# Two-layer GELU network on one core: the order of the first chunk's products, the order of waits, and w1's loads cut into more pieces

## The chip, the core and the metric

The kernel runs on one core of one Trainium2 chip. Its time is the device time of a run in microseconds (us); the time of a kernel is the median of its runs. A profile is one further execution, recorded by the hardware profiler. TensorE is called PE in the profile's rows (its weight loads PEld), VectorE DVE, ScalarE ACT, GpSimd POOL, SyncE SP; a q behind an engine's name is its queue of issues.

## The reference

```
h = einsum("bsd,df->bsf", x, w1) + b1
h = gelu(h)                      # tanh approximation
out = einsum("bsf,fd->bsd", h, w2) + b2
```

All arrays are bf16: x is 1 x 2048 x 448, w1 448 x 1792, w2 1792 x 448; out is 1 x 2048 x 448. So there are 2048 tokens, a model width of 448 = 3 x 128 + 64, and a hidden width of 1792 = 14 x 128.

## The kernel before

The tokens are worked in four chunks of 512. For each chunk, layer 1 makes g = gelu(x w1 + b1) with the hidden width on the partitions, 14 F-tiles of 128 in 7 pairs (`Layer1`, one object a pair); then layer 2 multiplies g with w2 (`Layer2`) and VectorE adds b2 on the way out of PSUM.

Every product uses half of TensorE's rows, 64, and products of the two halves are issued one after the other, so that they run side by side. For a pair of F-tiles the "a" products take one half of the rows for each F-tile, the "b" products the other half. The 448 rows of w1 are three slices (k = 0, 1, 2) of 128 and 64 last rows, which stand in a tile of their own, `w1r`, where VectorE copies them to the other half for the odd F-tiles (line 411, event `w1rU`). So a pair has 6 a products, 6 b products of the slices (`b_main`) and 2 of the last rows (`b_last`), after which ScalarE applies GELU (line 279). A pair accumulates in one of four PSUM units, used in turn; a unit is taken again when ScalarE has read it. `mm` (line 221) records every product. When the half changes within a bank, it adds a wait for the product before it in that bank.

x must be turned so that its width lies on the partitions. For chunks 1 to 3 DMA transposes do that. For chunk 0 TensorE does: x is loaded as it is (`xn`), turned in 64 x 64 blocks against an identity (`turn`, line 348) into PSUM, and drained to `xT` by VectorE (line 361) or ScalarE (line 359). A main turn (`turn_block`) is 4 instructions for one half of the chunk (h = 0 or 1, 256 tokens) and one slice k. `turn_first` makes five of the six and their drains, `turn_rest` the sixth, in unit 2, where the block of half 0 and slice 2 must have been drained first, and the turns of the last 64 columns, which are moved into both halves (`xR0`, two moves on VectorE and two on ScalarE).

The order of the work is written out by hand. `Program` keeps a list of instructions for each engine, with the events that each one waits for; `emit` turns those into semaphore waits in the order in which they are listed. TensorE's list for chunk 0 before the change: warm-up products, `turn_first`, pair 0's a products for half 0 of the tokens, `turn_rest`, pair 0's `b_main` over all tokens, pair 1's a, pair 0's a for half 1, pair 1's `b_main`, both `b_last`, pair 2's a, then for each next pair its a and the `b` of the one before.

w1 comes in blocks of whole F-tiles: blocks 0 and 1 (2 F-tiles each) from ScalarE's queue, block 2 (F-tiles 4 to 7) and block 3 (8 to 13) from SyncE's. SyncE's queue, in order: x, last rows piece 0 (F-tiles 0 to 3), block 2, last rows piece 1 (4 to 13), block 3, w2 in two halves, b2, then the twelve DMA transposes of the later chunks, and later the stores. A product waits for the block, and for the piece of last rows, that its F-tile lies in. Layer 2 of chunk 0 starts when pair 6 is done.

```
    W1CUTS = (0, 2, 4, 8, 14)
    RCUTS = (0, 4, 14)
    after = ["ident"] + after
    after += ([("xT0", h, k)] if k < KT else [("xR0", half, 0), ("xR0", half, 1)])
```

Of the kernel before, what the change touches and what calls it, by code (L numbers as in the profile page):

```python
# [77 lines left out]
def bass_standalone__dense_activation_gelu__prompt_kernel(  # L78
# [12 lines left out]
    SC = 512  # L91
    HC = SC // 2
# [4 lines left out]
    KT = 3  # L97
# [4 lines left out]
    with ExitStack() as es:  # L102
        sb = lambda name, shape, dt: es.enter_context(nc.sbuf_tensor(name, shape, dt))
        xn = sb("xn", [P, STC, D], BF16)
        xr = sb("xr", [P, STC // 2, P], BF16)
        ident = sb("ident", [P, P], BF16)
        xT = sb("xT", [P, KT + 1, S], BF16)
        w1_sb = sb("w1_sb", [P, KT, F], BF16)
        w1r = sb("w1r", [P, F], BF16)
# [14 lines left out]
        ones_m = one.broadcast_to([P, SC])  # L124


        W1CUTS = (0, 2, 4, 8, 14)

        def w1_of(ft):
            return max(i for i, c in enumerate(W1CUTS) if c <= ft)  # L130

        def load_w1(i, engine="sync"):
            c0, c1 = W1CUTS[i] * P, W1CUTS[i + 1] * P
            pr.dma(engine, lambda e: e.dma_start(  # L134
                w1_sb[:, :, c0:c1], w1[0:D3, c0:c1].rearrange("(k p) f -> p k f", p=P)), ("w1", i))

        RCUTS = (0, 4, 14)

        def load_w1r(i, engine="sync"):
            cs = slice(RCUTS[i] * P, RCUTS[i + 1] * P)  # L140
            pr.dma(engine, lambda e: e.dma_start(w1r[H:P, cs], w1[D3:D, cs]), ("w1r", i))  # L141

        def load_w2(a, b):
            pr.dma("sync", lambda e: e.dma_start(
                w2_sb[:, a:b, :], w2[a * P:b * P, :].rearrange("(f p) d -> p f d", p=P)), ("w2", a))
# [14 lines left out]
        load_w1(2)  # L160
        load_w1r(1)
        load_w1(3)
        load_w2(0, 7)
        load_w2(7, 14)
        pr.dma("sync", lambda e: e.dma_start(b2_bc[:, :], b2.partition_broadcast(P)), "b2")
        for c in range(1, NSC):
            for slot in range(KT + 1):
# [10 lines left out]
               after=["b1z"])  # L178
# [4 lines left out]
        def turn_b1():  # L183
            for q in range(4):
                pr.op("vector", lambda e, q=q: e.transpose(  # L185
                    b1t[32 * q:32 * q + 32, :], b1n[:, 32 * q:32 * q + 32]), after=["b1n"], event=("b1t", q))
            pr.op("vector", lambda e: e.tensor_copy(b1_f[:, :], b1t[:, 0:NFT]),
                  after=[("b1t", q) for q in range(4)], event="b1")
# [21 lines left out]
        def free(u):  # L210
            return [busy[(u, i)] for i in (0, 1, 2) if (u, i) in busy]

        def mm(u, lo, half, cols, lhsT, rhs, start, stop, after, event=None, skip=False):

            after = list(after)
            before = side.get((u, lo))
            if start:
                before = None
            if before is not None and before[0] != half:
                after.append(before[1])  # L220
            o = pr.op("tensor", lambda e: e.matmul(  # L221
                unit[u][:, lo, cols], lhsT=lhsT, rhs=rhs, start=start, stop=stop, skip_group_check=skip),
                after=after, event=event)
            side[(u, lo)] = (half, o)

        class Layer1:
# [6 lines left out]
            def step(self, part, k, t0=0, t1=SC):  # L233
                c, j, u = self.c, self.j, self.u
                s0 = c * SC
                for lo in (0, 1):
                    ft = 2 * j + lo
                    half = lo if part == "a" else 1 - lo
                    rows = slice(half * H, (half + 1) * H)
                    if k < KT:  # L240
                        lhsT = w1_sb[rows, k, ft * P:(ft + 1) * P]
                        after = [("w1", w1_of(ft))]
                    else:
                        lhsT = w1r[rows, ft * P:(ft + 1) * P]
                        after = [("w1r" if half else "w1rU", int(ft >= RCUTS[1]))]
                    if c == 0:
                        for h in range(t0 // HC, t1 // HC):
                            after += ([("xT0", h, k)] if k < KT else
                                      [("xR0", half, 0), ("xR0", half, 1)])
                    else:  # L250
                        after += [("xT", c), ("xTd", c)]
                    if self.fresh:
                        after += free(u)
                    fin = part == "b" and k == KT and t1 == SC
                    mm(u, lo, half, slice(t0, t1), lhsT, xT[rows, k, s0 + t0:s0 + t1], self.fresh, fin, after,
                       ("h", c, ft) if fin else None, self.skip)
                self.fresh = False
# [83 lines left out]
        def spot(u, i, rows=slice(0, P)):  # L341

            return unit[u][rows, :, i * H:(i + 1) * H].bitcast(BF16).rearrange("p b (t s) -> p b t s", t=2)

        def turn(o, i, event, after):

            for half, rows in enumerate(HALVES):
                pr.op("tensor", lambda e, half=half, rows=rows: e.transpose(o(half), i(rows), ident[rows, rows]),  # L348
                      after=["ident"] + after, event=event if half else None)

        def turn_block(h, k, u, i, wait=()):
            for t in (0, 1):
                turn(lambda half, t=t: spot(u, i)[:, half, t, :], lambda rows, t=t: xn[rows, 2 * h + t, k * P:(k + 1) * P],
                     ("xt", h, k) if t else None, ["x"] + list(wait))
# [9 lines left out]
        def drain_block(engine, h, k, u, i, after):  # L364
            move(engine,
                 lambda t: xT[:, k, h * HC:(h + 1) * HC].bitcast(t).rearrange("p (t b s) -> p b t s", b=2, t=2),
                 lambda t: unit[u][:, :, i * H:(i + 1) * H].bitcast(t).rearrange("p b (t s) -> p b t s", t=2),
                 [after], ("xT0", h, k))
            busy[(u, 0)] = ("xT0", h, k)

        def turn_first():
            pr.op("vector", lambda e: e.tensor_copy(  # L372
                xr[:, :, :].rearrange("p q (two h) -> p q two h", two=2),
                xn[:, :, D3:D].rearrange("p (q two) h -> p q two h", two=2)), after=["x"], event="xr_in")
            for k in (0, 2, 1):
                turn_block(0, k, k, 0)
                drain_block(("vector", "vector", "scalar")[k], 0, k, k, 0, ("xt", 0, k))
            for k in (0, 1):
                turn_block(1, k, 3, k)
            for k in (0, 1):  # L380
                drain_block("vector", 1, k, 3, k, ("xt", 1, 1))

        def turn_rest():


            turn_block(1, 2, 2, 0, [("xT0", 0, 2)])
            for q in range(STC // 2):
                turn(lambda half, q=q: spot(2, 1)[:, half, q, :], lambda rows, q=q: xr[rows, q, :], ("xr", q), ["xr_in"])
            drain_block("vector", 1, 2, 2, 0, ("xr", 1))
            for src, engine in enumerate(("vector", "scalar")):  # L390
                for dst in (src, 1 - src):
                    move(engine,
                         lambda t, src=src, dst=dst: xT[HALVES[dst], KT, 0:SC].bitcast(t).rearrange(
                             "p (q two b s) -> p b q two s", q=2, two=2, b=2)[:, :, :, src, :],
                         lambda t, src=src: unit[2][HALVES[src], :, H:2 * H].bitcast(t).rearrange(
                             "p b (q s) -> p b q s", q=2),
                         [("xr", 1), ("xT0", 1, 2)], ("xR0", dst, src))
            busy[(2, 1)] = ("xR0", 1, 0)
            busy[(2, 2)] = ("xR0", 0, 1)

        warm(NWARM)
        warm(1, HC)
        turn_first()
        L = [Layer1(0, j) for j in range(NPAIR)]
        L[0].a(0, HC)
        turn_rest()

        for i in (0, 1):
            odd = lambda rows, i=i: w1r[rows, RCUTS[i] * P:RCUTS[i + 1] * P].rearrange(
                "p (j two q) -> p j two q", two=2, q=P)[:, :, 1, :]  # L410
            pr.op("vector", lambda e, odd=odd: e.tensor_copy(odd(slice(0, H)), odd(slice(H, P))),  # L411
                  after=[("w1r", i)], event=("w1rU", i))
            if i == 0:
                turn_b1()
        L[0].b_main()
        L[1].a()
        L[0].a(HC, SC)
        L[1].b_main()
        for j in (0, 1):
            L[j].b_last()  # L420
# [6 lines left out]
        for c in range(NSC):  # L427
# [7 lines left out]
            else:  # L435

                for row in (0, H):
                    pr.op("vector", lambda e, row=row: e.tensor_copy(b2_z[row:row + 1, :], b2_bc[row:row + 1, :]),  # L438
                          after=["b2", "b2z0"], event="b2z" if row else None)
# [5 lines left out]
            if c + 1 < NSC:  # L445
                q = Layer2(c, 2)
# [7 lines left out]
            else:  # L454

                q, r = Layer2(c, 2, 0, DL), Layer2(c, 2, DL, D)
# [42 lines left out]
```

## Time and profile before

| | |
|---|---|
| median of 5 runs | 94.14 us (93.89 to 94.33) |
| the profiled execution's own time | 94.29 us |
| its span | 93.0 us |
| granted TensorE clock | 1.0 |
| TensorE busy, of the span | 89.1 us (96%) |
| ScalarE, VectorE busy | 38.1 us, 13.9 us |
| HBM read and written | 3.79 MB, 1.84 MB |

The page's times are from the start of the span. A row of the timeline has start, length, engine, line, operation and tiles; products overlap, so that a row's length holds the tail of its last one. The loads of the profiled execution, by the table of DMA issues: block 2 of w1 was issued at 2.88 us and landed 5.0 us later, piece 1 of the last rows was issued at 3.49 and landed 5.2 later, block 3 at 4.03 and 6.9 later, the halves of w2 at 4.66 and 5.20 and 9.1 later in the median. ScalarE's queue issued blocks 0 and 1 from 0.81 on, and they landed 3.9 later in the median. The issue of b2's broadcast held SyncE's queue for 3.67 us from 6.38 on.

### The profile page before, as it was taken

What the parts mean: (1) busy time and instruction counts of PE and PEld (TensorE: products, weight loads), DVE (VectorE), ACT (ScalarE), POOL (GpSimd) and SP (SyncE); (2) the same over time, 40 slices, a digit from 0 to 9 for tenths busy, and PEclk for the clock granted to TensorE, in tenths of its full rate; (3) what the DMA queues carried; (4) which work ended last, traced back from release to release, by engine and by line L of the source; (5) the groups of instructions that cost most, each with busy time, mean ns of one, the idle gap of its engine ahead of it and who ended that gap; (6) DMA issues with size and microseconds to landing.
All of it is one profiled execution on the core that took longest, in us unless ns stands there. A gap on an engine that the chain in (4) does not pass through costs nothing.

```text
span 93.0 us, 2058 instructions
## 1 busy us (share of the span) xinstructions
PE 89.1 (96%) x940; PEld 46.9 (50%) x940; DVE 13.9 (15%) x37; ACT 38.1 (41%) x63; POOL 1.7 (2%) x8
## 2 busy tenths in 40 slices
PE   6899799999999999999999999999999999999990
PEld 2355244555544444555544444455554444479990
DVE  0284002100433000000334000000233000000431
ACT  6135957700003787900002887900001878910011
POOL 6000000000000000000000000000000000000000
DMA  2999997555757000000033000000022000000023
GB/s 51 346 273 321 379 302 133 115 106 99 67 92 215 21 0 7 0 0 0 0 103 102 0 0 4 0 7 0 0 99 99 7 0 0 0 0 7 0 99 99
DMA packets 13000, 7.32 MB, mean 79 GB/s; under 512 B 7232, under 2 KB 12800, under 8 KB 12992
## 3 DMA queue, kind: packets, MB, share of 16 engines
q1 hardware_dynamic: 11888, 6.74, 29.4%
q10 hardware_dynamic: 1072, 0.46, 1.7%
q8 instruction: 7, 0.11, 0.5%
q14 instruction: 1, 0.01, 0.0%
q0 software_dynamic: 32, 0.00, 0.0%
HBM read 3.79 MB, written 1.84 MB: 60 GB/s over the span
## 4 chain that ended last, share of the span: by engine, by line
PE 86%; DMA 7%; SPq 2%; ACT 1%; ACTq 1%; issue 1%
PE u L221 86%; DMA w_sb<-in_w_dram 7%; SPq L141 1%; SPq L134 1%; ACTq L134 1%; ACT L179 1%; ACT out_sb L329 0%; ACT junk L179 0%
## 5 line engine op out<-in xcount | busy, mean ns | idle before, releaser
L279 ACT ACTIVATE g<-u,b_f 128x512 bf16<-128x512 f32 x56 | 34.8, 685 | 40.2 <-PE u L221 40.2
L221 PE MATMUL u<-w_sb,g 64*128 64x448 bf16 (+2 forms) x504 | 43.2, 328 | 0.0
L221 PE MATMUL u<-xT,w_sb 64*128 64x512 bf16 (+1 forms) x342 | 40.9, 372 | 0.8 <-DMA w_sb<-in_w_dram 0.5
L221 PEld LDWEIGHTS u<-w_sb,g 64*128 64x128 bf16 x504 | 25.7, 94 | 17.2
L221 PEld LDWEIGHTS u<-xT,w_sb 64*128 64x128 bf16 x342 | 16.6, 94 | 20.2 <-DMA w_sb<-in_w_dram 1.5
L332 DVE TENSOR_TENSOR out_sb<-u,b_bc 128x448 bf16<-128x448 f32 (+2 forms) x16 | 8.9, 592 | 63.7 <-PE u L221 63.7
L221 PE MATMUL u<-xT,w1r 64*128 64x512 bf16 x56 | 10.5, 376 | 0.0
L221 PEld LDWEIGHTS u<-xT,w1r 64*128 64x128 bf16 x56 | 2.8, 94 | 3.3
L329 ACT CAST out_sb<-u 128x320 bf16<-128x320 f32 (+1 forms) x2 | 0.7, 345 | 8.8 <-PE u L221 8.8
L196 PE MATMUL u<-const-bfloat16-1.0 128*128 128x512 bf16 (+1 forms) x8 | 3.1, 568 | 0.8 <-PEq L484 0.8
L359 ACT COPY xT<-u 64x256 bf16<-64x256 bf16 (+1 forms) x3 | 1.1, 369 | 3.3 <-PE u L348 2.1
L196 PEld LDWEIGHTS u<-const-bfloat16-1.0 128*128 128x128 bf16 x8 | 1.0, 139 | 2.4 <-issue 2.4
L361 DVE TENSOR_SCALAR xT<-u 128x128 uint32<-128x128 uint32 (+1 forms) x7 | 1.7, 285 | 0.5 <-PE u L348 0.4
L179 ACT ACT_TABLE_LOAD x1 | 1.3, 1283 | 0.8 <-PEq L484 0.8
L438 DVE COPY b_z<-b_bc 1x448 bf16<-1x448 bf16 x2 | 0.5, 267 | 6.3 <-DMA b_bc<-in_b_dram 6.3
L191 DVE COPY xT<-xT 64x512 bf16<-64x512 bf16 x3 | 0.9, 290 | 1.7 <-DMA xT<-in_x_dram 1.7
L348 PEld LDWEIGHTS u<-ident,xn 64*128 64x128 bf16 x24 | 0.6, 94 | 0.6 <-issue 0.6
L348 PE MATMUL u<-ident,xn 64*128 64x64 bf16 x24 | 0.7, 190 | 0.1
L185 DVE STREAM_TRANSPOSE b1t<-b1n 32x32 bf16<-32x32 bf16 x4 | 0.8, 202 | 0.1
L411 DVE COPY w1r<-w1r 64x256 bf16<-64x256 bf16 (+1 forms) x2 | 0.6, 289 | 1.0 <-DMA w1r<-in_w_dram 0.9
L372 DVE COPY xr<-xn 128x256 bf16<-128x256 bf16 x1 | 0.2, 227 | 3.0 <-DMA xn<-in_x_dram 3.0
L177 POOL DMA_DIRECT2D b1n<-in_b_dram x1 | 0.6, 647 | 0.0
(14 smaller groups left out, 2.6 us busy)
## 6 DMA issues: line engine op xcount, KB each, us to landing
w_sb<-in_w_dram SPq DMA_DIRECT2D x2, 784.0 KB, 9.1
out_dram<-out_sb SPq DMA_DIRECT2D x14, 112.0 KB, 1.7
w_sb<-in_w_dram SPq DMA_DIRECT2D x1, 576.0 KB, 6.9
xn<-in_x_dram SPq DMA_DIRECT2D x1, 448.0 KB, 3.2
w_sb<-in_w_dram ACTq DMA_DIRECT2D x2, 192.0 KB, 3.9
w_sb<-in_w_dram SPq DMA_DIRECT2D x1, 384.0 KB, 5.0
xT<-in_x_dram SPq DMA_TRANSPOSE x12, 3.6
w1r<-in_w_dram SPq DMA_DIRECT2D x1, 160.0 KB, 5.2
```

Of the source, the lines that this page charges most:

```text
L134: pr.dma(engine, lambda e: e.dma_start(w1_sb[:, :, c0:c1], w1[0:D3, c0:c1].rearrange("(k p) f -> p k f", p=P)), ("w1", i))
L141: pr.dma(engine, lambda e: e.dma_start(w1r[H:P, cs], w1[D3:D, cs]), ("w1r", i))
L179: pr.op("scalar", lambda e: e.activation(junk[:, :], one, ACT.Gelu_apprx_tanh), event="table")
L185: pr.op("vector", lambda e, q=q: e.transpose(b1t[32 * q:32 * q + 32, :], b1n[:, 32 * q:32 * q + 32]), after=["b1n"], event=("b1t", q))
L191: pr.op("vector", lambda e: e.tensor_copy(xT[0:H, KT, s0:s1], xT[H:P, KT, s0:s1]), after=after, event=event)
L196: pr.op("tensor", lambda e: e.matmul(unit[0][:, 0, 0:cols], lhsT=ones_w, rhs=ones_m[:, 0:cols], start=True, stop=True))
L221: o = pr.op("tensor", lambda e: e.matmul(unit[u][:, lo, cols], lhsT=lhsT, rhs=rhs, start=start, stop=stop, skip_group_check=skip), after=a ...
L279: pr.op("scalar", lambda e, lo=lo, ft=ft: e.activation(g[:, ft, c * SC:(c + 1) * SC], unit[u][:, lo, :], ACT.Gelu_apprx_tanh, bias=b1_f[:, ...
L332: pr.op("vector", lambda e, j=j, lo=lo: e.tensor_tensor(out=out_sb[:, j, d0:d1], in0=unit[u][:, lo, 0:d1 - d0], in1=b2_bc[:, d0:d1], op=AL ...
L348: pr.op("tensor", lambda e, half=half, rows=rows: e.transpose(o(half), i(rows), ident[rows, rows]), after=["ident"] + after, event=event i ...
L359: pr.op(engine, lambda e: e.copy(out(BF16), in_(BF16)), after=after, event=event)
L361: pr.op(engine, lambda e: e.tensor_single_scalar(out(U32), in_(U32), 0, ALU.bitwise_or), after=after, event=event)
```

## The change

The first chunk's work is put in another order: all six main turns stand together, the sixth in unit 3 beside the two others of half 1, and the three drains of half 1 wait for the last of these turns. Pair 0's a products follow for both halves of the tokens, with the turns of the last columns between slices 1 and 2 of half 1; then come pair 1's a, pair 0's `b_main`, pair 1's `b_main`, and on as before. Waits are listed in another order: of a product of chunk 0, the wait for the turned x ahead of the wait for w1; of a turn, the wait for x ahead of that for the identity. In the built kernels, of two waits of a product the one that is listed first is carried by the instruction itself, and the other stands in an instruction of its own ahead of it. Block 3 of w1 is cut in two (F-tiles 8 to 11 and 12 to 13), piece 1 of the last rows too (4 to 7 and 8 to 13), and SyncE's queue takes them by turns. VectorE makes three copies of the last rows instead of two.

```
--- before.py
+++ after.py
@@ -124,7 +124,7 @@
         ones_m = one.broadcast_to([P, SC])
 
 
-        W1CUTS = (0, 2, 4, 8, 14)
+        W1CUTS = (0, 2, 4, 8, 12, 14)
 
         def w1_of(ft):
             return max(i for i, c in enumerate(W1CUTS) if c <= ft)
@@ -134,7 +134,7 @@
             pr.dma(engine, lambda e: e.dma_start(
                 w1_sb[:, :, c0:c1], w1[0:D3, c0:c1].rearrange("(k p) f -> p k f", p=P)), ("w1", i))
 
-        RCUTS = (0, 4, 14)
+        RCUTS = (0, 4, 8, 14)
 
         def load_w1r(i, engine="sync"):
             cs = slice(RCUTS[i] * P, RCUTS[i + 1] * P)
@@ -160,6 +160,8 @@
         load_w1(2)
         load_w1r(1)
         load_w1(3)
+        load_w1r(2)
+        load_w1(4)
         load_w2(0, 7)
         load_w2(7, 14)
         pr.dma("sync", lambda e: e.dma_start(b2_bc[:, :], b2.partition_broadcast(P)), "b2")
@@ -242,11 +244,11 @@
                         after = [("w1", w1_of(ft))]
                     else:
                         lhsT = w1r[rows, ft * P:(ft + 1) * P]
-                        after = [("w1r" if half else "w1rU", int(ft >= RCUTS[1]))]
+                        after = [("w1r" if half else "w1rU", max(i for i, c in enumerate(RCUTS) if c <= ft))]
                     if c == 0:
                         for h in range(t0 // HC, t1 // HC):
-                            after += ([("xT0", h, k)] if k < KT else
-                                      [("xR0", half, 0), ("xR0", half, 1)])
+                            after = ([("xT0", h, k)] if k < KT else
+                                     [("xR0", half, 0), ("xR0", half, 1)]) + after
                     else:
                         after += [("xT", c), ("xTd", c)]
                     if self.fresh:
@@ -346,7 +348,7 @@
 
             for half, rows in enumerate(HALVES):
                 pr.op("tensor", lambda e, half=half, rows=rows: e.transpose(o(half), i(rows), ident[rows, rows]),
-                      after=["ident"] + after, event=event if half else None)
+                      after=after + ["ident"], event=event if half else None)
 
         def turn_block(h, k, u, i, wait=()):
             for t in (0, 1):
@@ -375,18 +377,17 @@
             for k in (0, 2, 1):
                 turn_block(0, k, k, 0)
                 drain_block(("vector", "vector", "scalar")[k], 0, k, k, 0, ("xt", 0, k))
-            for k in (0, 1):
+            for k in range(KT):
                 turn_block(1, k, 3, k)
-            for k in (0, 1):
-                drain_block("vector", 1, k, 3, k, ("xt", 1, 1))
+            for k in range(KT):
+                drain_block("vector", 1, k, 3, k, ("xt", 1, 2))
 
         def turn_rest():
 
 
-            turn_block(1, 2, 2, 0, [("xT0", 0, 2)])
             for q in range(STC // 2):
-                turn(lambda half, q=q: spot(2, 1)[:, half, q, :], lambda rows, q=q: xr[rows, q, :], ("xr", q), ["xr_in"])
-            drain_block("vector", 1, 2, 2, 0, ("xr", 1))
+                turn(lambda half, q=q: spot(2, 1)[:, half, q, :], lambda rows, q=q: xr[rows, q, :], ("xr", q),
+                     ["xr_in", ("xT0", 0, 2)])
             for src, engine in enumerate(("vector", "scalar")):
                 for dst in (src, 1 - src):
                     move(engine,
@@ -394,7 +395,7 @@
                              "p (q two b s) -> p b q two s", q=2, two=2, b=2)[:, :, :, src, :],
                          lambda t, src=src: unit[2][HALVES[src], :, H:2 * H].bitcast(t).rearrange(
                              "p b (q s) -> p b q s", q=2),
-                         [("xr", 1), ("xT0", 1, 2)], ("xR0", dst, src))
+                         [("xr", 1)], ("xR0", dst, src))
             busy[(2, 1)] = ("xR0", 1, 0)
             busy[(2, 2)] = ("xR0", 0, 1)
 
@@ -403,18 +404,20 @@
         turn_first()
         L = [Layer1(0, j) for j in range(NPAIR)]
         L[0].a(0, HC)
+        L[0].step("a", 0, HC, SC)
+        L[0].step("a", 1, HC, SC)
         turn_rest()
-
-        for i in (0, 1):
+        L[0].step("a", 2, HC, SC)
+
+        for i in range(3):
             odd = lambda rows, i=i: w1r[rows, RCUTS[i] * P:RCUTS[i + 1] * P].rearrange(
                 "p (j two q) -> p j two q", two=2, q=P)[:, :, 1, :]
             pr.op("vector", lambda e, odd=odd: e.tensor_copy(odd(slice(0, H)), odd(slice(H, P))),
                   after=[("w1r", i)], event=("w1rU", i))
             if i == 0:
                 turn_b1()
+        L[1].a()
         L[0].b_main()
-        L[1].a()
-        L[0].a(HC, SC)
         L[1].b_main()
         for j in (0, 1):
             L[j].b_last()
```

More of the change, by code (lines that the diff above doesn't have):

```diff
@@ L124, in bass_standalone__dense_activation_gelu__prompt_kernel @@
         ones_m = one.broadcast_to([P, SC])
-        W1CUTS = (0, 2, 4, 8, 14)
+        W1CUTS = (0, 2, 4, 8, 12, 14)
         def w1_of(ft):
@@ L135, in load_w1 @@
                 w1_sb[:, :, c0:c1], w1[0:D3, c0:c1].rearrange("(k p) f -> p k f", p=P)), ("w1", i))
-        RCUTS = (0, 4, 14)
+        RCUTS = (0, 4, 8, 14)
         def load_w1r(i, engine="sync"):
@@ L162, in bass_standalone__dense_activation_gelu__prompt_kernel @@
         load_w1(3)
+        load_w1r(2)
+        load_w1(4)
         load_w2(0, 7)
@@ L244, in step @@
                         lhsT = w1r[rows, ft * P:(ft + 1) * P]
-                        after = [("w1r" if half else "w1rU", int(ft >= RCUTS[1]))]
+                        after = [("w1r" if half else "w1rU", max(i for i, c in enumerate(RCUTS) if c <= ft))]
                     if c == 0:
                         for h in range(t0 // HC, t1 // HC):
-                            after += ([("xT0", h, k)] if k < KT else
-                                      [("xR0", half, 0), ("xR0", half, 1)])
+                            after = ([("xT0", h, k)] if k < KT else
+                                     [("xR0", half, 0), ("xR0", half, 1)]) + after
                     else:
@@ L348, in turn @@
                 pr.op("tensor", lambda e, half=half, rows=rows: e.transpose(o(half), i(rows), ident[rows, rows]),
-                      after=["ident"] + after, event=event if half else None)
+                      after=after + ["ident"], event=event if half else None)
         def turn_block(h, k, u, i, wait=()):
@@ L377, in turn_first @@
                 drain_block(("vector", "vector", "scalar")[k], 0, k, k, 0, ("xt", 0, k))
-            for k in (0, 1):
+            for k in range(KT):
                 turn_block(1, k, 3, k)
-            for k in (0, 1):
-                drain_block("vector", 1, k, 3, k, ("xt", 1, 1))
+            for k in range(KT):
+                drain_block("vector", 1, k, 3, k, ("xt", 1, 2))
         def turn_rest():
-            turn_block(1, 2, 2, 0, [("xT0", 0, 2)])
             for q in range(STC // 2):
-                turn(lambda half, q=q: spot(2, 1)[:, half, q, :], lambda rows, q=q: xr[rows, q, :], ("xr", q), ["xr_in"])
-            drain_block("vector", 1, 2, 2, 0, ("xr", 1))
+                turn(lambda half, q=q: spot(2, 1)[:, half, q, :], lambda rows, q=q: xr[rows, q, :], ("xr", q),
+                     ["xr_in", ("xT0", 0, 2)])
             for src, engine in enumerate(("vector", "scalar")):
@@ L396, in turn_rest @@
                              "p b (q s) -> p b q s", q=2),
-                         [("xr", 1), ("xT0", 1, 2)], ("xR0", dst, src))
+                         [("xr", 1)], ("xR0", dst, src))
             busy[(2, 1)] = ("xR0", 1, 0)
@@ L405, in bass_standalone__dense_activation_gelu__prompt_kernel @@
         L[0].a(0, HC)
+        L[0].step("a", 0, HC, SC)
+        L[0].step("a", 1, HC, SC)
         turn_rest()
-        for i in (0, 1):
+        L[0].step("a", 2, HC, SC)
+        for i in range(3):
             odd = lambda rows, i=i: w1r[rows, RCUTS[i] * P:RCUTS[i + 1] * P].rearrange(
@@ L414, in bass_standalone__dense_activation_gelu__prompt_kernel @@
                 turn_b1()
+        L[1].a()
         L[0].b_main()
-        L[1].a()
-        L[0].a(HC, SC)
         L[1].b_main()
```

## The prediction

> **What bounds the kernel now.** I read the split by engines first, then the chain that ended last, then the waits of TensorE, and last the start of the timeline piece by piece.
>
> ```profile
> PE 89.1 (96%) x940; PEld 46.9 (50%) x940; DVE 13.9 (15%) x37; ACT 38.1 (41%) x63; POOL 1.7 (2%) x8
> ```
> ```profile
> 4.03 6.88 DMA w_sb<-in_w_dram
> 10.91 0.05 issue
> 10.95 79.92 PE u L221 x847
> 90.88 0.02 issue
> ```
>
> TensorE (PE) is the bound. From 10.95 us to 90.88 us the chain of waits is one unbroken run of 847 products, in which nothing else ended last. Ahead of it the chain is a transfer: a piece of w1 that landed at 10.91. So the change, which touches only the first chunk of tokens, can gain only as much as it brings the 10.95 forward, and everything behind moves with it unless a new wait appears. TensorE's rows of this stretch (start, length, engine, line, operation, then in brackets the idle time before it and what ended that):
>
> ```profile
> 4.07 0.47 PE L348 MATMUL u<-ident,xn 64*128 64x64 bf16 x20
> 4.77 0.50 PE L221 MATMUL u<-xT,w_sb 64*128 64x256 bf16 x6 [0.24 <-DVE xT L361]
> 5.11 0.23 PE L348 MATMUL u<-ident,xn 64*128 64x64 bf16 x4
> 5.17 0.23 PE L348 MATMUL u<-ident,xr 64*128 64x64 bf16 x4
> 5.42 2.45 PE L221 MATMUL u<-xT,w_sb 64*128 64x512 bf16 x24
> 7.69 0.61 PE L221 MATMUL u<-xT,w1r 64*128 64x512 bf16 x4
> 8.12 2.12 PE L221 MATMUL u<-xT,w_sb 64*128 64x512 bf16 x18
> 10.06 0.40 PE L221 MATMUL u<-xT,w1r 64*128 64x512 bf16 x2
> 10.95 1.47 PE L221 MATMUL u<-xT,w_sb 64*128 64x512 bf16 x12 [0.50 <-DMA w_sb<-in_w_dram]
> 12.26 0.38 PE L221 MATMUL u<-xT,w1r 64*128 64x512 bf16 x2
> 12.47 1.46 PE L221 MATMUL u<-xT,w_sb 64*128 64x512 bf16 x12
> 13.77 0.38 PE L221 MATMUL u<-xT,w1r 64*128 64x512 bf16 x2
> ```
>
> Prices first. Two 64-row products run side by side as a pair, so I count starts, not durations. Seven pairs of 512 columns take 1.51 us in the undisturbed part (from the row at 12.26 to that at 13.77), 0.216 us a pair. A pair of 256 columns follows the one before in 0.11 us, and a pair of turns in 0.029 us (ten pairs from 4.07 to about 4.36). The stretch 4.07 to 10.95 holds 24 pairs' worth of 512 columns, 5.18 us, and 14 pairs of turns, 0.41 us: 5.59 of 6.88 us. The other 1.29 us are three holes: 4.36 to 4.77 (0.41, the turned x must be drained), 5.23 to 5.42 (0.19, the b products follow the a products of the same banks and wait for them), and 10.28 to 10.95. This last one is 10.06 + 0.216 = 10.28 against 10.95, 0.67 us: pair 4 wants w1's block 3. The rest is rounding.
>
> **The change, part by part.**
>
> *Turns and first products.* No product and no turn is added or taken away; 24 main turns now stand together. Two more pairs move into the first hole (4.36 + 0.06 = 4.42), so they cost nothing; without that hole they would cost 0.06. The drains are the next limit:
>
> ```profile
> 4.34 0.89 DVE L361 TENSOR_SCALAR xT<-u 128x128 uint32<-128x128 uint32 x4 [0.16 <-PE u L348]
> 5.49 0.92 DVE L361 TENSOR_SCALAR xT<-u 128x128 uint32<-128x128 uint32 x3 [0.27 <-PE u L348]
> ```
>
> VectorE's four drains start 0.20 us apart and take 0.28 each, so the third, fourth and the new fifth start at 4.74, 4.94, 5.14 and end at 5.02, 5.22, 5.43. That they now wait for the last of three blocks (turned by about 4.63) is hidden by the drain ahead, which holds VectorE until 4.74. What waits for a drain starts about 0.07 after its end (the weight load at 5.83, shown below, after the drain of 5.49 ended near 5.78). TensorE in the new order: first half of pair 0 at 4.77, 4.88, 5.00; second half, slice 0, at 5.11 (drain done at 5.02); slice 1 at 5.22 + 0.07 = 5.29; the turns of the last rows, 5.40 to 5.46; slice 2 at 5.43 + 0.07 = 5.50. Pair 1's a products start at 5.61 (w1's block 1, 192 KB in the table of DMA issues, landed by about 5.3). From there: three pairs to 6.26, pair 0's b to 6.91, pair 1's b to 7.55, two last pairs to 7.99. The 0.19 hole is gone, since pair 1's a products lie between a and b of pair 0. That puts pair 2 at 7.99 instead of 8.12, 0.13 sooner. The moves of the last rows start near 5.66 instead of 5.81 and must be done by 7.55; before they ended near 6.6. No cost.
>
> *The order of the waits.* An instruction with two waits spends one in an instruction of its own ahead of it. Before, that was the late one: the drain ended near 4.63, the weight load came at 4.74. With the late wait on the product the 0.11 may become 0.05. I expect 0.06 at the first turn and 0.06 at the first product (both sides: 0 to 0.14 in sum; a loss has no reason, the number of waits is the same). Pair 2 could then be ready at 7.87. But:
>
> ```profile
> 5.83 1.54 PEld L221 LDWEIGHTS u<-xT,w_sb 64*128 64x128 bf16 x20 [0.30 <-DVE xT L361]
> 7.47 0.33 PEld L221 LDWEIGHTS u<-xT,w1r 64*128 64x128 bf16 x4
> 7.97 1.77 PEld L221 LDWEIGHTS u<-xT,w_sb 64*128 64x128 bf16 x18 [0.17 <-DMA w_sb<-in_w_dram]
> ```
>
> The weight load of pair 2, the third row, waited for w1's block 2 until 7.97 already, hidden behind the last products of pair 1. Its transfer is issued and sized as before, so pair 2 starts no sooner than about 8.00. I count nothing for the waits and 0.12 for the whole early part.
>
> *Pairs 2 and 3* are ten pairs: 8.00 + 2.16 = 10.16. With block 3 there in time, pair 4 starts then, 0.79 sooner than 10.95.
>
> *w1 in more pieces.* Block 3 shrinks from 576 to 384 KB, and the last rows ahead of it from 160 to 64 KB. In the old order block 2 landed about 7.93, the second piece of last rows about 8.72 (VectorE's copy of it starts at 8.74), block 3 at 10.91: 736 KB in 2.98 us. In proportion, the 448 KB now in their place take 1.81 us and block 3 lands at 9.74. That is one end. The other: a load lands with the last of its 16 DMA engines, and the packet records show that one engine is behind, with a single packet of block 3 lasting 1.29 us (8.00 to 9.29) before the rest ran at 0.061 us per 1,536 bytes. If that pause comes at the same time again, only the bytes of that one engine go away: 1/16 of 288 KB, 18 KB at 1,536 bytes in 0.061 us = 0.73 us, and the landing is 10.91 - 0.73 = 10.18, weight load at 10.22. So pair 4 starts between 10.16 and 10.23. I take 10.19: gain 0.76 us. Late next would be either, TensorE's own work or block 3, within 0.07 of each other.
>
> Here the Trainium skill speaks against the change. "DMA: Bandwidth & Descriptors", section "Anatomy of one DMA — SWDGE (gpsimd) path", gives about 2.0 us fixed plus bytes at 436 GB/s for a DMA by itself on the GpSimd path, and its section "Bandwidth" tells to batch to 1 MiB. The change adds two DMAs. By the rule taken in series, the last block lands at 10.91 + 4.0 = 14.9. The trace has DMAs one behind the other on SyncE's queue: 160 KB landed 0.8 us after the load ahead. A fixed 2 us is not paid in series there, and the measurement decides: the last block lands about 10.9 to 11.1. As for shorter rows (now 512 bytes at the least), packets of 512 and 1,024 bytes of this trace took 27 and 46 ns in the median, 19 and 22 bytes per ns: 24 packets per engine of the last block cost an estimated 0.1 us more. I keep 0 to 0.3.
>
> *New waits.* Pair 4's last rows (third piece) are wanted 2.8 us after pair 4 starts, at 13.0; by the order of the queue they land about 10.4, and the copy takes below 0.36. That copy now stands in VectorE's line ahead of the bias copy, which waited for its own transfer until 15.44. Pair 6 wants the last block 3.02 us (14 pairs) after pair 4, at 13.2: slack over 2 us.
>
> *SyncE's queue.* Two more issues of 0.5 to 0.6 us each stand ahead of both halves of w2, b2's broadcast and twelve transposes. The w2 issues at 4.66 and 5.20 landed 9.1 us later in the median, since the data wait behind w1; a later issue is hidden. The halves landed near 13.0 and 15.0; layer 2 starts at 16.36 - 0.76 = 15.6 and reaches the second half seven feature tiles later, 16.9. If the broadcast's issue (3.67 us[...]) and the transposes slip by 1.2 us: chunk 1 wants its x at 26.2, and its transposes are issued from 10.09 on, landing 3.6 us after issue. No cost.
>
> **Sum.** The profiled execution took 94.29 us, of which the span is 93.0. 94.29 - 0.76 = 93.53. It lies 0.15 above the median of 94.14; if those 0.15 are part of the wait that goes, the new time stays 93.5, otherwise it is 93.4. I say 93.5.
>
> **Rivals.**
> 1. *As worked out* (chance 0.62): 93.35 to 93.65, predicted 93.5.
> 2. *The lagging DMA engine still sets the pace* (0.22). Blocks 2 and 3 come late by a few tenths, and part of the 0.67 stays. For it: the stall stood behind one slow packet, and runs differ by 0.44. Against: the smaller block leaves less to move. With half of the stall left: 94.14 - 0.76 + 0.34 = 93.7; with nearly all of it, 93.95.
> 3. *Block 2 lands sooner* (0.11). Then the waits' 0.13 counts too: 94.14 - 0.79 - 0.13 = 93.2. Against: its transfer is unchanged.
> 4. *Slower: the added DMAs are paid in series* (0.05). The last block lands at 14.9, pair 6 starts at 14.95 instead of 13.2, 1.75 late: 94.29 - 0.76 + 1.75 = 95.3. It decides from a landing of 13.15 on, and is slower than before from 13.9. Against: the landings above.
> 5. That the changed order does nothing on TensorE is excluded: the instruction lists of the two builds differ as the diff says, and the waits changed places. If it bought nothing early, pair 2 stays at 8.12 and pair 4 starts at 10.28: 93.6, inside case 1.
>
> **How the numbers follow.** A measurement of this kernel can tell about 0.3% from no change, 0.28 us: faster means below 93.86, slower above 94.42. Case 1, case 3 and about 0.14 of case 2 are faster: 0.87. The rest of case 2 is the same, 0.08; case 4 slower, 0.05. The range from 93.2 to 93.85 takes in cases 1 and 3 and the better part of 2; some 0.15 lie outside.
>
> **What would show it.** Right: pair 2's first weight load still ends a wait for w1 near 8.0; the row of w1r products that now starts at 10.06 starts near 9.94, and the next row 0.22 later with no wait for w1; from there an unbroken run of products, as long as before. Wrong: a wait for w1 of more than 0.1 us at pair 4 or pair 6, a wait for w2 near 16, or a hole over 0.1 us between 5.1 and 5.6.

## The result and the profile after

| | before | after |
|---|---|---|
| median | 94.03 us (93.66 to 94.54, 73 runs) | 93.66 us (93.30 to 94.28, 38 runs) |
| ratio to before | 1 | 0.9966, 95% interval 0.9956 to 0.9975 |
| profiled execution, span | 94.29 us, 93.0 us | 93.62 us, 92.3 us |

The change saves 0.32 us (94.03 x 0.0034), between 0.24 and 0.41 by the interval. That is half of the 0.64 that was forecast, and less than the spread of either kernel's runs (0.9 and 1.0), so only the medians of many runs show it. The two profiled executions lie 0.67 apart, so each of them must be asked how far it stands for the usual run.

The chain of waits of the changed kernel (start, length, what), its first piece and its longest, has no transfer in it any more, the pieces left out included:

```profile
0.78 3.36 PE u L198 x8
...
5.78 84.42 PE u L223 x891
```

TensorE's own rows of the same execution, and one weight load:

```profile
4.08 0.77 PE L350 MATMUL u<-ident,xn 64*128 64x64 bf16 x24
4.76 0.97 PE L223 MATMUL u<-xT,w_sb 64*128 64x256 bf16 x10
...
8.13 2.11 PE L223 MATMUL u<-xT,w_sb 64*128 64x512 bf16 x18
10.07 0.38 PE L223 MATMUL u<-xT,w1r 64*128 64x512 bf16 x2
10.29 1.46 PE L223 MATMUL u<-xT,w_sb 64*128 64x512 bf16 x12
```
```profile
7.97 1.77 PEld L223 LDWEIGHTS u<-xT,w_sb 64*128 64x128 bf16 x18 [0.17 <-DMA w_sb<-in_w_dram]
```

Pair 4 starts at 10.29, 0.22 us behind its neighbour, with no wait for w1: the 0.67 us are gone. But pair 2 starts at 8.13, not at 8.00, no sooner than in the profile of before. The reason is in the group of the turns (count, then busy us and mean ns of one), first of the changed kernel, then of before:

```profile
L350 PE MATMUL u<-ident,xn 64*128 64x64 bf16 x24 | 0.8, 232 | 0.0
```
```profile
L348 PE MATMUL u<-ident,xn 64*128 64x64 bf16 x24 | 0.7, 190 | 0.1
```

The same turns took 232 ns in the mean in place of 190. Pairs of turns followed at 0.053 us up to 4.60, in place of 0.029: TensorE ran at about half speed that long, and the clock record of this execution begins its full rate at 4.67 (the clock "opens" there, as I call it from here on). The profile's granted clock reads 1.0 ahead of that too, so the pace has to tell it. In the profile of before the warm-up products follow one another at 0.427 us up to 3.30, and the next start comes 0.35 us later. At full rate such products follow at 0.216, so an estimated 0.27 of these 0.35 us were still slow, and the clock opened at about 3.57, ahead of the first turn. The two profiles differ by more than the change.

### The profile page after: what moved, and what is told of

Same layout as the page of the kernel before. It is cut to its first block, busy times and chain, and to the rows that moved or that the text cites. A ratio compares the mean times of both kernels' runs of the same rounds, so it can differ in the third digit from the quotient of the medians.

```text
span 92.3 us, 2059 instructions
## 1 busy us (share of the span) xinstructions
PE 89.4 (97%) x940; PEld 46.8 (51%) x940; DVE 14.1 (15%) x38; ACT 38.1 (41%) x63; POOL 1.7 (2%) x8
## 4 chain that ended last, share of the span: by engine, by line
PE 97%; ACT 0%; issue 0%
PE u L223 92%; PE u L198 4%; PE u L350 1%; ACT out_sb L331 0%
```

## The experiments

Before the first runs I held three theories. 1: the wait for block 3 is all there is to gain, and it is shorter than 0.67 in a usual execution. 2: it is 0.67, but block 3 is still late in many executions after. 3: the cuts bring 0.7 and the new order costs 0.3. Ratios below are to before on the same chip.

### The parts one by one

**cuts_only**: the kernel before with `W1CUTS = (0, 2, 4, 8, 12, 14)`, `RCUTS = (0, 4, 8, 14)`, the two loads more and the third copy.

> Only the finer cuts of w1 and its last rows are made, order and waits stay as before. Theory 1 (the wait for block 3 is all there is to gain, and in a usual execution it is shorter than the 0.67 us of the profile of before, since TensorE's clock opens later there and TensorE comes later to it): 0.997 of before, within 0.001 of the whole change. Theory 2 (the wait is 0.67 us in usual executions too, but block 3 is still late in many executions of the changed kernel): also about 0.997, with a wait for w1 at pair 4 in the profile. Theory 3 (the cuts bring the full 0.7 us and the new order costs 0.3 us early on): 0.993, clearly faster than the whole change.

Measured: 93.92 us, ratio 1.0006 (0.9985 to 1.0027). At most 0.14 us of gain, none by the middle. All three theories had put a gain here.

**order_only**: the changed kernel with the old cuts and loads.

```
-        W1CUTS = (0, 2, 4, 8, 12, 14)
+        W1CUTS = (0, 2, 4, 8, 14)
...
-        RCUTS = (0, 4, 8, 14)
+        RCUTS = (0, 4, 14)
...
-        load_w1r(2)
-        load_w1(4)
...
-        for i in range(3):
+        for i in (0, 1):
```

> New order and new order of waits, old cuts. Theories 1 and 2: pair 4 waits for the same block 3 as before, so 1.000 of before, within 0.001. Theory 3: 1.000 as long as the wait covers the early loss, at most 1.003. If the order brings the gain after all: 0.997.

Measured: 93.93 us, ratio 0.9984 (0.9962 to 1.0005). Not told apart from no change, nor from the whole gain.

**after_old_waits**: the changed kernel with the waits listed as before.

```
-                            after = ([("xT0", h, k)] if k < KT else ...) + after
+                            after += ([("xT0", h, k)] if k < KT else ...)
...
-                      after=after + ["ident"], ...
+                      after=["ident"] + after, ...
```

> The whole change but for the order of the waits, which stays as before. By the prediction the order of waits is worth 0 to 0.14 us of early time, hidden behind block 2: 0.9966 to 0.998 of before. If the waits are the gain: 1.000.

Measured: 93.76 us, ratio 0.9973 (0.9955 to 0.9992). By the middle of the interval most of the gain is there without the new order of waits. With order and cuts together there is a gain that neither showed alone: this kernel lies 0.17 us under order_only, although order_only has the better waits (their runs overlap, 93.54 to 93.90 and 93.52 to 94.11).

**before_no_block3**: the wait for block 3 taken out of the kernel before, by other weights.

```
-                        lhsT = w1_sb[rows, k, ft * P:(ft + 1) * P]
-                        after = [("w1", w1_of(ft))]
+                        wf = ft - 6 if c == 0 and ft >= 8 else ft
+                        lhsT = w1_sb[rows, k, wf * P:(wf + 1) * P]
+                        after = [("w1", w1_of(wf))]
```

> The kernel before, but pairs 4 to 6 of the first chunk multiply by the weights of F-tiles 2 to 7 in place of 8 to 13 for their three slices, so that nothing in chunk 0 waits for block 3 (which is loaded all the same); the first chunk's values for those F-tiles are not the reference's. It measures the wait for block 3 in usual executions. Theory 1: 0.3 us goes, 0.997 of before. Theories 2 and 3: the 0.67 us of the profile goes, 0.993. In its profile no wait for w1 is seen after pair 2.

Measured: 94.03 us, ratio 1.0007 (0.9985 to 1.0028). With no wait for block 3 in it at all, the kernel before is as slow as with it. All three theories fall: in the median of the runs there is at most 0.14 us of this wait to take away. Its profile shows how that can be (TensorE's rows, then the group of its turns):

```profile
4.16 0.72 PE L349 MATMUL u<-ident,xn 64*128 64x64 bf16 x20
...
8.69 2.12 PE L221 MATMUL u<-xT,w_sb 64*128 64x512 bf16 x18
10.63 0.39 PE L221 MATMUL u<-xT,w1r 64*128 64x512 bf16 x2
10.85 1.02 PE L221 MATMUL u<-xT,w_sb 64*128 64x512 bf16 x7
```
```profile
L349 PE MATMUL u<-ident,xn 64*128 64x64 bf16 x24 | 1.1, 238 | 0.0
```

The turns took 238 ns in the mean. The product that starts at 5.87 is followed 0.335 us later, so that by the working above the clock opened near 6.1. TensorE itself comes to pair 4 at 10.85, where before it was let go at 10.95: with a clock as late as this, a block 3 as late as that of the profile of before (10.91) would have cost 0.1 us and not 0.67. But block 3 was not that late here. It landed at 9.75, ahead of the 10.28 at which pair 4 is ready under an early clock. So the wait takes two things at once, an early clock and a late landing, and this execution had neither.

New theory: the change gains by the order of products and waits alone, on TensorE's own path ahead of pair 2; the cuts matter only in an execution where the clock opens early and block 3 is late. To see it, the clock's chance had to be taken out.

### With the first turn held back

```
-    NWARM = 7
+    NWARM = 15
...
+        for i in range(8):
+            pr.op("scalar", lambda e, i=i: e.activation(hold[:, i, :], ones_m, ACT.Gelu_apprx_tanh),
+                  after=["x"] if i == 7 else [], event="late" if i == 7 else None)
...
-                     ("xt", h, k) if t else None, ["x"] + list(wait))
+                     ("xt", h, k) if t else None, ["late"] + list(wait))
```

Four kernels have this edit, on the kernel before, on the changed one, on after_old_waits, and on the kernel before with only its products reordered:

```
-        L[0].b_main()
+        L[0].a(HC, SC)
         L[1].a()
-        L[0].a(HC, SC)
+        L[0].b_main()
         L[1].b_main()
```

> The kernel before, with 15 long warm-up products in place of 7 and with its first turn held back by eight made-up activations on ScalarE (into a tile of its own), to about 7.4 us; the output is unchanged. By then TensorE's clock is open in every execution and w1 has landed. Theory 1 (the clock opens at a chance point of each execution[...] and what TensorE does before that runs at half speed): all runs lie within 0.3 us of each other, where those of before spread over 0.9; the time is that of a warm before without a wait for block 3, moved by 3.3 us: 96.9, within 0.2. If the spread comes from the transfers or from the end of the kernel, it stays near 0.9.

> The same hold on the changed kernel. Neither the clock nor w1's landings matter, so the difference from before_held is what the new order is worth on a warm TensorE. By the prediction's sum 0.13 us for the products and about 0.06 for the first product's wait: 0.13 to 0.20 us faster than before_held. If the new order costs time (theory 3): slower than before_held by up to 0.3. If it is worth the 0.32 us that was measured in all: 0.32 faster.

> The same hold on the changed kernel with the order of the waits of before. The difference from after_held is what the order of the waits is worth at the first product (the first turn's wait is another one here): 0.06 us by the prediction, 0.00 if the wait is no dearer in an instruction of its own.

> The same hold on the kernel before with its turns, drains and waits as they were, and only the products in the new order: pair 0's a products for the second half of the tokens, then pair 1's a, then pair 0's b. The hole of 0.19 us between a and b of pair 0 goes, but the sixth block is drained late (5.78 in the profile of before), so slice 2 of the second half waits for it: 0.05 faster to 0.15 slower than before_held. If the turns' place doesn't matter, it is as fast as after_old_waits_held.

| held kernel | runs, us | median | first turn, pair 2 (us in the profile) |
|---|---|---|---|
| before_held | 96.06 to 96.10, one of 96.71 | 96.07 | 6.54, 10.60 |
| after_old_waits_held | 95.91 to 96.15 | 95.93 | 6.53, 10.44 |
| after_held | 95.83 to 95.84 | 95.84 | 6.44, 10.35 |
| products_only_held | 96.25 to 96.29 | 96.26 | 6.53, 10.77 |

The activations follow one another in 0.52 us, so the turn came at 6.54 and not at the 7.4 that I had worked out; 2.48 us after the profile of before in place of 3.3. The time is then 94.29 - 0.67 + 2.48 = 96.10, against 96.07 measured. The spread shrinks from 0.73 (the 11 runs of before beside them) to some hundredths, but for one run of 96.71 and two of after_old_waits_held at 96.1. The hold hides the landings of x and w1 as well as the clock, so this alone doesn't say how the spread divides between them, and it can't show what the cuts are worth.

On this quiet ground the order is worth 96.07 - 95.84 = 0.23 us, and it divides: 0.14 for turns and products (before_held to after_old_waits_held), 0.09 for the waits. First before_held, then after_held:

```profile
6.54 0.47 PE L352 MATMUL u<-ident,xn 64*128 64x64 bf16 x20 [0.37 <-ACT hold L184]
7.25 0.50 PE L225 MATMUL u<-xT,w_sb 64*128 64x256 bf16 x6 [0.24 <-DVE xT L365]
7.59 0.23 PE L352 MATMUL u<-ident,xn 64*128 64x64 bf16 x4
7.65 0.23 PE L352 MATMUL u<-ident,xr 64*128 64x64 bf16 x4
7.90 2.45 PE L225 MATMUL u<-xT,w_sb 64*128 64x512 bf16 x24
...
10.60 2.12 PE L225 MATMUL u<-xT,w_sb 64*128 64x512 bf16 x18
```
```profile
6.44 0.52 PE L354 MATMUL u<-ident,xn 64*128 64x64 bf16 x24
7.06 0.88 PE L227 MATMUL u<-xT,w_sb 64*128 64x256 bf16 x10
7.78 0.22 PE L354 MATMUL u<-ident,xr 64*128 64x64 bf16 x4
7.86 2.23 PE L227 MATMUL u<-xT,w_sb 64*128 64x256 bf16 x20
...
10.35 2.11 PE L227 MATMUL u<-xT,w_sb 64*128 64x512 bf16 x18
```

The last activation of the hold ended at 6.40 in before_held and at 6.39 in after_held; the turn follows 0.15 and 0.06 us behind it, so that it comes 0.09 sooner where it carries that wait itself. From the first turn to pair 2 it is 4.06 us before and 3.91 after: the hole ahead of the row at 7.90 has gone, less what the drains of half 1 cost. In after_old_waits_held this stretch is 3.91 too. The first product does start sooner in after_held, 0.62 us after the first turn where it is 0.71 there, but nothing of that is left at pair 2: the drains set the pace behind it.

In products_only_held the sixth block is still turned late. The row of the products says what they wait for, with VectorE's drains below it:

```profile
8.27 2.23 PE L225 MATMUL u<-xT,w_sb 64*128 64x256 bf16 x20 [0.20 <-DVE xT L365]
```
```profile
6.80 0.88 DVE L365 TENSOR_SCALAR xT<-u 128x128 uint32<-128x128 uint32 x4 [2.39 <-PE u L352]
7.92 0.93 DVE L365 TENSOR_SCALAR xT<-u 128x128 uint32<-128x128 uint32 x3 [0.24 <-PE u L352]
```

Slice 2's products wait for the drain that starts at 7.92. This kernel is 0.19 slower than before_held, a little more than the 0.15 that I had allowed; the new order of products pays only together with the turns' new place.

### With the loads shifted too

The loads were to move with the turn, so that the landings count again while the clock is open: activations on ScalarE ahead of x's load and of w1's, and 16 warm-up products.

```
-    NWARM = 7
+    NWARM = 16
...
+        pr.barrier("sync", ["hold3"])
         pr.dma("sync", lambda e: e.dma_start(xn[:, :, :], x0v), "x")
-        pr.barrier("sync", ["table"])
+        pr.barrier("sync", ["hold4"])
```

> The kernel before with everything that loads x and w1 moved back together by about 3.6 us: x and the pieces of w1 and of its last rows are issued behind made-up activations on ScalarE, at the same distances from each other as before, under 16 long warm-up products in place of 7; the output is unchanged. TensorE's clock is then open before the first turn in every execution, as it was in the profile of before, but the transfers still set block 2's and block 3's landings. It measures how much of the wait for block 3 a usual execution has when the clock opens early. If the 0.67 us of the profile of before is usual with an early clock: 94.3 + 3.6 = 97.9. If it was an unlucky landing: 97.3 to 97.6, and the spread of the runs is that of the landings.

> The same shift on the changed kernel. 0.23 us less than before_shifted from the order of products and waits, and less by the whole of before_shifted's wait for block 3: 0.9 us less if that is the 0.67 of the profile, 0.3 to 0.5 less if it was an unlucky landing. Block 2 may hold it where the prediction put it, at 8.00 plus the shift.

> The same shift on the kernel with the finer cuts alone. What the cuts are worth with an early clock: before_shifted's wait for block 3 goes, 0.1 to 0.6 us less than before_shifted. If the cuts are worth nothing even then: as before_shifted.

> The same shift on the kernel with the new order of products and waits and the old cuts. Pair 4 is ready 0.23 us sooner and meets the same block 3: as before_shifted where block 3 is late, up to 0.23 less where it isn't. If block 3 never matters: 0.23 less than before_shifted, as after_shifted.

| | median, us (lowest to highest) | x landed to first turn | first turn to pair 4 |
|---|---|---|---|
| before_shifted | 97.55 (97.45 to 97.89) | 0.13 | 6.22 |
| cuts_shifted | 97.42 (97.30 to 97.83) | 0.14 | 6.21 |
| order_shifted | 97.33 (97.18 to 97.42) | 0.05 | 6.07 |
| after_shifted | 97.21 (97.03 to 97.58) | 0.05 | 6.06 |

These runs answer less than they were made for. SyncE's loads of w1 started 0.52 us after x's (4.85 and 4.33 in before_shifted), not 1.53 as before, so every one of these kernels issued block 3 about 1 us sooner after x than before. In before_shifted's profile pair 4 follows with no wait:

```profile
13.91 0.40 PE L227 MATMUL u<-xT,w1r 64*128 64x512 bf16 x2
14.13 0.61 PE L227 MATMUL u<-xT,w_sb 64*128 64x512 bf16 x4
```

That "an unlucky landing" is favoured by 97.55 is therefore not proof. What they show: in the last two columns the order brings 0.15 and the wait 0.08 to 0.09 again, 0.23 to 0.24 in all, and the cuts nothing. The medians' 0.13 for the cuts alone lies inside the spread of six runs, and so does the 0.12 between order_shifted and after_shifted.

What stands about the landing is the time from issue to landing of block 3. In the seven profiles with the old cuts it is 6.9 us in before, then in order_only, before_no_block3, before_held, products_only_held, before_shifted and order_shifted 6.2, 5.7, 6.4, 5.5, 6.1 and 6.4. Issued at 4.03, block 3 must land in 6.2 to be there for pair 4 at 10.28. The profile of before holds the longest of the seven, and an early clock too. The rows of block 3 in before and in before_no_block3 (issues, KB, us to landing):

```profile
w_sb<-in_w_dram SPq DMA_DIRECT2D x1, 576.0 KB, 6.9
```
```profile
w_sb<-in_w_dram SPq DMA_DIRECT2D x1, 576.0 KB, 5.7
```

In the seven profiles with the new cuts block 3's first piece took 5.2 to 5.4, so the cuts do bring it sooner and more evenly. Block 2, which was not cut, took 4.1 to 5.1 in those and 4.8 to 5.4 in the others.

## Why the prediction was right or wrong

The time lay in the range and the direction held; the size did not, and the main term, taken alone, is not what the change gains. That 93.66 lies in the range is in part luck: the case as worked out ended at 93.65, and the range went further up only to take in a transfer that still lags, which is not what was found.

- **The wait for block 3, 0.67 us.** This is the step that failed. It was real in the profile, and it is not in the profile after, but before_no_block3 (1.0007) and cuts_only (1.0006) show that in the median there is at most 0.14 of it to gain. I read one execution as the usual one; it had an early clock and the latest landing of seven. The warning lay in the numbers at hand: an execution with 0.67 us of waiting stood only 0.15 above the median.
- **The turns' pace, 0.029 us a pair.** Taken from one execution in the same way. In the six profiles of kernels without a hold or a shift, mean turns of 190, 190, 232, 236, 237 and 238 ns show two clocks that opened ahead of the turns and four that opened during or after them. No step of the sum had the clock in it.
- **The early part, 0.13 us for turns and products.** Right: 0.14 held, 0.15 shifted. The drains' steps held as well: pair 2 comes 3.91 us after the first turn, where the working had 7.99 - 4.07 = 3.92.
- **The order of the waits.** I took 0.06 at the turn and 0.06 at the product and counted nothing, since pair 2's weight load, which waited for block 2 until 7.97, would hide it. Measured: 0.09 at the turn, of the product nothing that reaches pair 2, and the 0.09 shows in the time on a quiet start. Block 2 does hold pair 2 in some executions (in the profile of order_only it starts at 8.28, where the products ahead of it would have let it go at 8.17), but not in the profile after.
- **More DMAs, later issues, new waits.** No cost is seen: the changed kernel's pair 4 and pair 6 wait for nothing, and rival 4 is out. Block 3's first piece landed at 9.40 and the last at 10.32, ahead of both ends of the working (9.74 and 10.18) and of its 10.9.
- **Rivals.** Rival 2 has the right number (93.7) for another reason: not a lagging transfer after the change, but little waiting before it.

Order and waits give 0.23 us on a quiet start; the change as a whole 0.24 to 0.41. Whether the rest, 0.01 to 0.18, is the wait for block 3 in the executions that have it, or a larger gain under a late clock, stays open. So does whether the 0.23 is there in a usual start without the cuts: order_only measured 0.15 (from a loss of 0.05 to a gain of 0.36), and the kernels that have both order and cuts lie lower. The new order wants blocks 2 and 3 sooner, so the finer cuts may be worth nothing with the old order and something with the new one; no run here settles that, since the hold hides the landings and the shift issued block 3 about 1 us sooner after x.

## What to carry to other kernels

Ahead of a gain that is read from one profile's wait, ask whether the same execution had an early or a late clock, and how late its transfer landed: the mean duration of one small product and the time from issue to landing, compared with other profiles of that kernel, tell it in two rows. A wait in the first microseconds is worth what taking it away saves in the median of many runs, and one kernel with the wait removed by other data settles that before any transfer is tuned. To measure some tenths of a microsecond in a start that varies by nine tenths, hold both kernels back behind the same made-up work and compare them there.

## What the runs showed of the hardware

The clock opened at about 3.57 us in one profile, at 4.67 in another and near 6.1 in a third, with the same products ahead of it from 0.78 us on. The second is a clock record, the others are worked out above from the pace of the products; in after_shifted, which has a record (4.47), the same working (0.377 us between two starts) gives 4.47 too. The other four records have 3.75, 4.14, 4.16 and 4.68. The Trainium skill, "TensorE: Matmul & The Clock Gate", section "Part 1: The HAM clock gate (the "warmup" mystery)", has a free-running window of 3.4 us, so that the point varies from run to run, and puts it around 4 us into sustained products with 0.5 us to either side. That it varies agrees; here it came 2.8 to 5.3 us after the first product, which is wider than the page has it, and 2.8 and 3.0 (the record of 3.75) are sooner than its 3.4 us of sustained work. There the measurement decides. The page puts the cost of the slow start at under 1% of a typical span and advises against fitting a count of slow products; here the whole change is 0.34%.

A wait in an instruction of its own ahead of the waiting one cost 0.08 to 0.09 us more than the same wait on the instruction itself: from the end of that wait to the first turn it took 0.15 us in before_held and 0.06 in after_held, 0.13 to 0.14 and 0.05 in the shifted kernels. In the packet records single packets of a load took 1.3 us where the median of their size is 0.05 to 0.07, in the profile of before in block 3 and in that of the changed kernel in block 2.
